# Two transformer layers on one core: full matmuls in column tiles, a square on GpSimd, Q's copies in one operation, a fifth pair

## The chip, the cores and the metric

The kernel runs on one NeuronCore of a Trainium2 chip. The core has a matrix engine (TensorE, PE in the profile; PEld is its loading of weights), VectorE (DVE), ScalarE (ACT), GpSimd (POOL) and the DMA queues, of which SyncE (SP) issues most. The metric is device time in microseconds (us), the median of several executions.

## The reference

Two identical layers, each an attention block and a feed-forward block, on 2048 rows of 512 columns in bf16. Both passes use the same weights.

```python
x = A_x                                   # [1, 2048, 512]
x = x + attention(layernorm(x), wqkv, wo)  # 32 heads of 16 columns
x = x + relu(layernorm(x) @ w1) @ w2       # w1 [512, 1792], w2 [1792, 512]
x = x + attention(layernorm(x), wqkv, wo)
x = x + relu(layernorm(x) @ w1) @ w2

# attention, for each head:
scores = (q @ k.T) * 16 ** -0.5            # 2048 x 2048
o = softmax(scores) @ v
```

There are 2 x 32 x 2048 x 2048 exponentials, 268 million. With 128 partitions working side by side that is 2,097,152 columns of one element per partition.

## The kernel before

Keys lie on the partitions. One matmul makes 128 keys x 512 queries of scores for one head; heads have only 16 columns, so four matmuls of 32 rows each (a head and its neighbour, with Q's copy masked so that the neighbour counts zero) sit in the array side by side. Three such blocks fill a slot of three PSUM banks (`ps_s`), and there are two slots in turn. A block of scores then goes one of two ways.

Most go through ScalarE's exponential, a whole slot of 1536 columns at once, or 1024 columns if VectorE takes the third block:

```python
ex = nc.scalar.activation(
    out=eb[:, 0 : place[m]], in_=b[:, 0 : place[m]], func=ACTF.Exp,
    scale=1.0 / (LOG2E * UNIT),
)
if half is not None:
    dve_block(half, taken, b[:, place[m] : W * QS], ex, recent)
```

The third block of some slots goes to VectorE, which makes the exponential by bit arithmetic. Two blocks make a pair. The scores become 16-bit integers that read as bf16 are a straight-line approximation (`lin`), once per block. Then a chain works on the whole pair of 1024 columns: it takes the mantissa (`step`), squares it (`power`, in the tile `cube`), takes the exponent (again into `step`), and multiplies. `lin`, `step` and `cube` all go to the second matmul with the values, which adds them up.

```python
first = nc.vector.tensor_scalar(                 # dve_block, once per block, reads PSUM
    out=lin[which][:, half * QS : (half + 1) * QS], in0=src, scalar1=EXP_BIAS,
    scalar2=0.0, op0=ALU.add, op1=ALU.max,
)
...
def bits(keep, put):                             # chain, once per pair
    nc.vector.tensor_scalar(
        out=stair, in0=line, scalar1=keep, scalar2=put, op0=ALU.bitwise_and,
        op1=ALU.bitwise_or,
    )

mantissa = stair.bitcast(BF16)
steps = (
    (342, lambda: bits(0x7F, 0x3F80)),
    (609, lambda: nc.vector.tensor_mul(out=power, in0=mantissa, in1=mantissa)),
    (342, lambda: nc.vector.tensor_scalar(       # left out for most pairs
        out=power, in0=power, scalar1=CUBE, scalar2=None, op0=ALU.mult)),
    (342, lambda: bits(0x7F80, 0)),
    (609, lambda: nc.vector.tensor_mul(
        out=power.bitcast(BF16), in0=power, in1=line.bitcast(BF16))),
)
```

How many pairs are lent to VectorE is decided while the program is built. The kernel's Python keeps a model of when each engine will be free (the first numbers in `steps` are nanoseconds of VectorE) and writes the instructions of each engine in the order that the model finds. A new pair is begun only if fewer than `NP` pairs are under way and its chain (`CHAIN`) would end in time:

```python
elif (not pairs or pair_no[0] + 1 - pairs[0]["n"] < NP) and (...):
    queued = sum(t["cost"] for t in dve_q if "chain" in t)
    ...
    ends = max(now_dve[0] + others, now_pe[0] + 2600.0) + SPREAD * (queued + CHAIN)
```

All other matmuls (Q, K, V, the output projection and the feed-forward block) go between those of attention and use the whole 128 x 128 array. Q is copied out of PSUM twice, with one mask for each of the two heads that share 32 rows.

```python
nc.tensor.matmul(out, lhsT, rhs, start=i % k == 0, stop=i % k == k - 1)   # mm_group

nc.tensor.matmul(                                # pv: values, four column tiles of 32
    ps_o[32 * g : 32 * g + 32, 0 : sg["w"]],
    values[:, 4 * sg["T"] + g, 2 * e : 2 * e + 32],
    rhs, start=g not in sg["begun"], stop=not sg["rem"][g],
    tile_position=(0, 32 * g), skip_group_check=True,
)

def q_masked(n, b, e, w=QS):
    return nc.vector.tensor_scalar(
        out=qbuf[n % 2][e][:, 0:w], in0=b, scalar1=qmask[e][:, 0:1], scalar2=None,
        op0=ALU.mult,
    )
```

GpSimd has little to do: it sets constants at the start, refines the layernorm's reciprocal square root on tiles of 4 columns, and issues the DMAs that spread a row of sums over partitions.

Of the kernel before, what the change touches and what calls it, by code (L numbers as in the profile page):

```python
# [11 lines left out]
FP32 = mybir.dt.float32  # L12
BF16 = mybir.dt.bfloat16
# [4 lines left out]
ALU = mybir.AluOpType  # L18
# [6 lines left out]
def kernel(  # L25
# [10 lines left out]
    nc = tc.nc  # L36
    P = 128
# [12 lines left out]
    QS = 512  # L50
    NQS = S // QS
    TPC = QS // P
    NT = 8
    SCALE = float(DH) ** -0.5
# [11 lines left out]
    LOG2E = 1.4426950408889634  # L66
    UNIT = 128.0
    EXP_BIAS = (127.0 - math.log2(SUM)) * UNIT
    CHAIN = 2500.0
    NP = 4  # L70
    NC = 3
    THIRD = (8, 9, 10, 11)

# [1 line left out]
    SWITCH = 105.0  # L75
# [3 lines left out]
    C_LAG, R_LAG, U_LAG = 3600.0, 10500.0, 3000.0  # L79
    VLAG = 1  # L80
    RSTD_LAG = 5000.0
    AHEAD = (8.0, 8.0)
    LATE = 0.0
    MID = 2
# [15 lines left out]
    def sb(shape, dt, name):  # L100
        return persist.tile(shape, dt, name=name)

    ident = sb([P, P], BF16, "ident")
    mask = [sb([P, 1], FP32, f"mask{e}") for e in range(2)]
    qmask = [sb([P, 1], FP32, f"qmask{e}") for e in range(2)]
    wqkv = sb([P, NDC, 3 * D], BF16, "wqkv")
    wo = sb([P, NDC, D], BF16, "wo")
    w1buf = [sb([P, NDC, P], BF16, f"w1_{n}") for n in range(NW1)]
# [16 lines left out]
    va2 = [sb([P, 2, H // 2, PW], BF16, f"vaug0_{n}") for n in range((NKB - TPC) // 2)]  # L125
# [11 lines left out]
    ot = [sb([P, QS], BF16, f"ot{t}") for t in range(NT)]  # L137
# [9 lines left out]
    acc0 = [x[:].bitcast(FP32).rearrange("p a b -> p (a b)") for x in htp]  # L147
    acc0.append(kt1[:].bitcast(FP32).rearrange("p a b -> p (a b)"))
    ebuf = [sb([P, W * QS], BF16, f"e{n}") for n in range(NE)]
    qbuf = [[sb([P, QS], BF16, f"q{n}_{e}") for e in range(2)] for n in range(2)]  # L150
    ubuf = [sb([P, QS], FP32, f"u{n}") for n in range(NU)]
    rbuf = [sb([P, QS], FP32, f"r{n}") for n in range(NU)]
    cbuf = [sb([P, QS // 32], FP32, f"c{n}") for n in range(NU)]
    xnbuf = [sb([P, D], BF16, f"xn{n}") for n in range(TPC)]
    stats = [sb([P, nc.vector.BN_STATS_DIM], FP32, f"stats{n}") for n in range(2)]
    mv = [sb([P, TPC, nc.vector.BN_AGGR_DIM], FP32, f"mv{n}") for n in range(2)]
    va_ = [sb([P, TPC], FP32, f"va{n}") for n in range(2)]
    ya_ = [sb([P, TPC], FP32, f"ya{n}") for n in range(2)]
    ta_ = [sb([P, TPC], FP32, f"ta{n}") for n in range(2)]
    warm = sb([P, 1], FP32, "warm")  # L160

    ps_s = [psum.tile([P, W, QS], FP32, name=f"ps_s{n}") for n in range(2)]
# [54 lines left out]
    def uses(ins, bank, makes=None, needs=None):  # L217

        tile, w = bank
        log = users.setdefault(tile, deque(maxlen=40))
        for other, ow, made_there in log:
            if (
                ow != w and other.engine != ins.ins.engine
                and (needs is None or made_there != needs)
            ):
                tc.declare_no_dep(ins.ins, other, reason="different PSUM banks")
        log.append((ins.ins, w, makes))
# [2 lines left out]

    now_pe = [0.0]
    now_dve = [0.0]
    mode = [None]
    busy = [0.0]
    bank_free = [0.0]
# [2 lines left out]
    def mark(key, engine="dve", lag=0.0):  # L240
        made[key] = (engine, (now_pe if engine == "pe" else now_dve)[0] + lag)

    def at(keys, engine):
# [10 lines left out]
            t = max(t, when)  # L254
        return t

    def pe_start(kind, ready=0.0):
        return max(now_pe[0] + (SWITCH if mode[0] != kind else 0.0), ready)

    def pe_run(kind, units, ready=0.0):  # L260
        now_pe[0] = pe_start(kind, ready) + units * MM
        mode[0] = kind
        busy[0] += units * MM

    def dve_run(cost, ready=0.0):
        now_dve[0] = max(now_dve[0], ready) + cost
# [33 lines left out]

    def do_piece():
        c, fn, ready = cur.popleft()
        pe_run("f", c, ready)
        fn()
        owed[0] -= c

# [111 lines left out]
    def mm_group(mms, fin, makes, deps, per=1, cost=EVAC, after=None, wide_by=QS, sums=1):  # L418


        hold = {}
        pieces = []
        n = len(mms)
        for a in range(0, n, per):

            def piece(a=a):
                if a == 0:
                    hold["b"] = bank()[:, 0 : sums * wide_by]
                b = hold["b"]
                for i in range(a, min(a + per, n)):  # L430
                    lhsT, rhs = mms[i]
                    k = n // sums
                    out = b[:, i // k * wide_by : (i // k + 1) * wide_by]
                    nc.tensor.matmul(out, lhsT, rhs, start=i % k == 0, stop=i % k == k - 1)  # L434
                if a + per >= n:
                    put_evac(cost, lambda: fin(b))
                    if after:
                        after()

            pieces.append((min(per, n - a) * wide_by / QS, piece))  # L440
        return group(pieces, makes, deps)
# [51 lines left out]
    def ln_newton(tag):  # L493

        n = ln_n(tag)
        a, y, t1 = va_[n][:], ya_[n][:], ta_[n][:]
        for _ in range(3):
            nc.gpsimd.tensor_mul(out=t1, in0=y, in1=y)
            nc.gpsimd.tensor_mul(out=t1, in0=t1, in1=a)
            nc.gpsimd.tensor_scalar(  # L500
                out=t1, in0=t1, scalar1=-0.5, scalar2=1.5, op0=ALU.mult, op1=ALU.add
            )
            nc.gpsimd.tensor_mul(out=y, in0=y, in1=t1)
# [117 lines left out]
            (wqkv[:, c, T * P : (T + 1) * P], xnT[xj][:, c, a : a + w]) for c in range(NDC)  # L621
        ]

    def q_masked(n, b, e, w=QS):
        return nc.vector.tensor_scalar(  # L625
            out=qbuf[n % 2][e][:, 0:w], in0=b, scalar1=qmask[e][:, 0:1], scalar2=None,
            op0=ALU.mult,
        )

    def q_group(n, l, j, T):  # L630
        xj, _, w = columns(l, j)
        cost = 133 + 1.045 * w

        def fin(b):
            q_masked(n, b, 0, w)
            evac.appendleft((cost, 0.0, lambda: (q_masked(n, b, 1, w), mark(("q", n)))))

        return mm_group(
            q_mms(l, j, T), fin, [("q", n)], each(TPC, "xnT", ("ln1", l, xj)), cost=cost,
            wide_by=w,  # L640
        )
# [151 lines left out]
    def finish_segment(sg, last):  # L793
# [40 lines left out]

        def mul(a, w):
            nc.vector.scalar_tensor_tensor(  # L836
                out=ot[t][:, at_column + a : at_column + a + w], in0=u[:, a : a + w], scalar=mask[e][:, 0:1],
                in1=r[:, a : a + w], op0=ALU.mult, op1=ALU.mult,
            )
            for i in range(a // P, (a + w) // P):  # L840
                mark(("ot", l, j, t, i))
# [189 lines left out]
    def chain(p):  # L1031
        key, n = p["key"], p["n"]
        line, stair, power = lin[n % NP][:], step[n % NC][:], cube[n % NC][:]

        def bits(keep, put):
# [3 lines that stand above are left out]
            )  # L1039

        mantissa = stair.bitcast(BF16)
        p["scaled"] = all(
            ("third", sg["l"], kb) in made for us in p["blocks"] for sg, kb, g in us
        )
        steps = (
            (342, lambda: bits(0x7F, 0x3F80)),
            (609, lambda: nc.vector.tensor_mul(out=power, in0=mantissa, in1=mantissa)),  # L1047
            (342, lambda: nc.vector.tensor_scalar(
                out=power, in0=power, scalar1=CUBE, scalar2=None, op0=ALU.mult)),
            (342, lambda: bits(0x7F80, 0)),  # L1050
            (609, lambda: nc.vector.tensor_mul(  # L1051
                out=power.bitcast(BF16), in0=power, in1=line.bitcast(BF16))),
        )
        nos = (0, 1, 3, 4) if p["scaled"] else range(5)
        for n, after in zip(nos, (None,) + tuple(nos)):
            cost, fn = steps[n]
            k = key + (n,) if n + 1 < len(steps) else key
            early = [("added", p["n"] - NC)] if p["n"] > NC else []
            task(cost, fn, [k], [key + (after,)] if n else early)
            maker[k]["chain"] = p  # L1060
# [11 lines left out]
    idle_matmuls(18)  # L1072
    for e in range(2):
        nc.vector.tensor_reduce(
            out=mask[e][:],
            in_=ident[:].rearrange("p (g e d) -> p e g d", g=4, e=2)[:, e],
            op=ALU.add, axis=mybir.AxisListType.XY,
        )
        nc.vector.tensor_scalar(
            out=qmask[e][:], in0=mask[e][:], scalar1=SCALE * LOG2E * UNIT, scalar2=None,  # L1080
            op0=ALU.mult,
        )
    for i in range(TPC):
# [24 lines left out]
    uses(nc.scalar.copy(out=ktp[0][0][0][:], in_=b), in_bank[0])  # L1108
    mark(("k", 0, 0, 0))
    b = plain(q_mms(0, 0, 0))  # L1110
    for e in range(2):
        uses(q_masked(0, b, e), in_bank[0])
    mark(("q", 0))
    for kb in range(2):
        b = plain(v_mms(kb))
# [57 lines left out]
    while units:  # L1173
# [123 lines left out]
        for _ in range(times):  # L1297
            pe_run("s", 1, s_ready)
            for a, (sg, kb, g) in sorted(zip(place, now), key=in_turn):
                kt = ktp[sg["l"]][sg["T"]][kb // TPC]  # L1300
                kc = (kb % TPC) * P
                nc.tensor.matmul(  # L1302
                    b[:, a : a + sg["w"]],
                    kt[32 * g : 32 * g + 32, kc : kc + P],
                    qbuf[sg["n"] % 2][sg["e"]][32 * g : 32 * g + 32, 0 : sg["w"]],
                    start=True, stop=True, tile_position=(32 * g, 0),
                )
        m = len(now) - len(taken)
# [160 lines left out]
```

The softmax here doesn't subtract the row's maximum and nothing guards it: scores larger than these inputs give would overflow.

## Time and profile before

| | us |
|---|---|
| median of 3 executions | 1614.96 |
| lowest, highest | 1613.95, 1618.53 |
| span of the profiled execution | 1611.5 |
| exponentials on ScalarE run from | 16.8 to 1577.9 |
| granted TensorE clock (mean) | 0.997 |

A busy time in the profile is the time in which an engine had an instruction under way. Instructions overlap at their ends, so the sum of single durations is larger than the busy time of the group. A matmul's duration includes its way through the array, and four that sit side by side count once each. In a line of a group, the number after the bar is the busy time in us, then the mean duration of one in ns, then the idle time of the engine before them and what ended it. Line numbers are those of the kernel before: L1302 are the score matmuls, L901 the ones with the values, L434 the full-array ones, L1311 the exponential, L995 the step `lin`, L1036 both bit operations, L1047 the square, L1051 the last multiplication, L625 Q's copies.

### The profile page before, as it was taken

To read this page: it belongs to the slowest core of one execution; us is meant where nothing else is said; L and a number is where in the kernel's file an instruction comes from. 1 tells how busy PE (TensorE), PEld (TensorE's weight loads), DVE (VectorE), ACT (ScalarE), POOL (GpSimd) and SP (SyncE) were. 2 spreads that over 40 slices of the span, in tenths; PEclk is the share of its full clock that TensorE was granted. 3 is DMA by queue.
4 is the path that set the end of the run, shared out by engine and by line. 5 is a ranking of instruction groups with operands and counts; after the bars stand their busy time and mean duration, and the time that the engine had idled before them with its cause. 6 is when DMAs were issued, how large, how long until landed. Compare 5 with 4: busy or idle time off the path is not lost.

```text
span 1611.5 us, 35252 instructions
## 1 busy us (share of the span) xinstructions
PE 1451.6 (90%) x14667; PEld 508.9 (32%) x14863; DVE 1496.8 (93%) x3007; ACT 1566.0 (97%) x1387; POOL 93.8 (6%) x279
## 2 busy tenths in 40 slices
PE   8888888999989999899998998888989999899997
PEld 3222222322222222222222222222333333344444
DVE  7669999999999999999898998999999999999994
ACT  6999999999999999999999999999999999999993
POOL 2000001001010011000100000001001010010100
PEclk9999999999999999999999999999999999999999
DMA  5000000210002100021000100000210111121223
GB/s 164 1 1 2 2 2 10 46 28 12 5 18 45 21 15 9 12 47 25 9 1 17 31 1 1 2 3 9 44 30 16 26 29 36 22 48 36 47 46 73
DMA packets 113889, 39.97 MB, mean 25 GB/s; under 512 B 103328, under 2 KB 111264, under 8 KB 113728
## 3 DMA queue, kind: packets, MB, share of 16 engines
q1 hardware_dynamic: 101696, 26.21, 7.1%
q0 software_dynamic: 10688, 10.18, 3.4%
q8 instruction: 116, 1.90, 0.5%
q10 hardware_dynamic: 1344, 1.31, 0.2%
q14 instruction: 45, 0.37, 0.1%
HBM read 24.38 MB, written 2.10 MB: 16 GB/s over the span
## 4 chain that ended last, share of the span: by engine, by line
ACT 78%; PE 11%; DVE 7%; issue 3%; DMA 1%; ACTq 0%; DVEq 0%
ACT e L1311 78%; PE ps_s L1302 4%; PE ps_o L901 3%; PE ps_f L434 3%; DVE lin L995 2%; DVE step L1036 1%; PE ps_s L1365 1%; DVE cube L1047 1%; DVE cube L1051 1%; DVE stats L465 0%; DVE ht L682 0%; DVE q L625 0%; DVE ot L836 0%; DVE x L708 0%; DMA c<-u 0%
## 5 line engine op out<-in xcount | busy, mean ns | idle before, releaser
L1311 ACT ACTIVATE e<-ps_s 128x1024 bf16<-128x1024 f32 (+1 forms) x1366 | 1554.8, 1367 | 6.6 <-PE ps_s L1302 4.7
L1302 PE MATMUL ps_s<-q,ktp 32*128 32x512 bf16 (+1 forms) x6060 | 601.2, 341 | 106.7 <-ACT e L1311 84.7
L901 PE MATMUL ps_o<-e,vaug 128*32 128x512 bf16 (+1 forms) x4284 | 494.7, 345 | 11.3 <-DVE u L823 4.8
L995 DVE TENSOR_SCALAR lin<-ps_s 128x512 int16<-128x512 f32 x662 | 452.6, 686 | 35.8 <-PE ps_s L1302 30.4
L1302 PEld LDWEIGHTS <-ktp 32*128 32x128 bf16 x6060 | 189.9, 91 | 504.5 <-issue 375.6
L1036 DVE TENSOR_SCALAR step<-lin 128x1024 int16<-128x1024 int16 x662 | 262.9, 420 | 3.3 <-PE ps_o L901 0.6
L901 PEld LDWEIGHTS <-vaug 128*32 128x32 bf16 x6004 | 161.5, 94 | 302.2 <-issue 291.5
L1047 DVE TENSOR_TENSOR cube<-step 128x1024 f16<-128x1024 bf16 x331 | 225.9, 685 | 2.7
L1051 DVE TENSOR_TENSOR cube<-cube,lin 128x1024 bf16<-128x1024 f16 x331 | 225.5, 682 | 0.0
L901 PE MATMUL ps_o<-step,vaug 128*32 128x512 bf16 (+1 forms) x836 | 143.2, 340 | 0.3 <-issue 0.3
L901 PE MATMUL ps_o<-cube,vthird 128*32 128x512 bf16 (+1 forms) x788 | 138.2, 337 | 0.6 <-issue 0.3
L901 PE MATMUL ps_o<-lin,vaug 128*32 128x512 bf16 (+1 forms) x836 | 127.4, 338 | 4.1 <-DVE u L823 2.8
L434 PE MATMUL ps_f<-xnT,w 128*128 128x512 bf16 (+1 forms) x446 | 116.9, 345 | 5.6 <-issue 2.5
L434 PE MATMUL ps_f<-w,ht 128*128 128x512 bf16 x334 | 104.8, 384 | 5.6 <-issue 4.3
L850 POOL DMA_DIRECT2D r<-u x52 | 37.5, 721 | 1165.9 <-DVE step L1036 424.3
L434 PE MATMUL ps_f<-xnT,wqkv 128*128 128x512 bf16 (+1 forms) x288 | 82.3, 359 | 6.4 <-issue 2.5
L682 DVE TENSOR_SCALAR ht<-ps_f 128x512 bf16<-128x512 f32 x103 | 70.7, 687 | 3.2 <-PE ps_f L434 3.0
L434 PE MATMUL ps_f<-wo,ot 128*128 128x512 bf16 x206 | 65.4, 384 | 3.0 <-issue 1.9
L625 DVE TENSOR_SCALAR q<-ps_f,qmask 128x512 bf16<-128x512 f32 (+1 forms) x102 | 64.8, 661 | 3.1 <-PE ps_f L434 3.0
L434 PEld LDWEIGHTS <-w 128*128 128x128 bf16 x504 | 39.1, 97 | 60.0 <-issue 50.6
L836 DVE SCALAR_TENSOR_TENSOR ot<-u,mask,r 128x512 bf16<-128x512 f32 (+2 forms) x82 | 51.3, 627 | 1.1
L901 PEld LDWEIGHTS <-vthird 128*32 128x32 bf16 x788 | 39.8, 95 | 32.8 <-issue 30.1
(91 smaller groups left out, 609.8 us busy)
## 6 DMA issues: line engine op xcount, KB each, us to landing
w<-in_B_w_dram SPq DMA_DIRECT2D x140, 128.0 KB
r<-u POOLq DMA_DIRECT2D x25, 256.0 KB, 7.1
r<-u POOLq DMA_DIRECT2D x27, 128.0 KB, 4.5
out_dram<-x SPq DMA_DIRECT2D x16, 128.0 KB
x<-in_A_x_dram SPq DMA_DIRECT2D x14, 128.0 KB
w<-in_B_w_dram SPq DMA_DIRECT2D x1, 1792.0 KB
wqkv<-in_A_wqkv_dram ACTq DMA_DIRECT2D x2, 512.0 KB
c<-u SPq DMA_DIRECT2D x48, 8.0 KB
```

The costliest lines, as they stand in the source:

```text
L434: nc.tensor.matmul(out, lhsT, rhs, start=i % k == 0, stop=i % k == k - 1)
L625: return nc.vector.tensor_scalar(out=qbuf[n % 2][e][:, 0:w], in0=b, scalar1=qmask[e][:, 0:1], scalar2=None, op0=ALU.mult,)
L682: nc.vector.tensor_scalar(out=out, in0=sums, scalar1=0.0, scalar2=None, op0=ALU.max)
L836: nc.vector.scalar_tensor_tensor(out=ot[t][:, at_column + a : at_column + a + w], in0=u[:, a : a + w], scalar=mask[e][:, 0:1], in1=r[:, a ...
L850: nc.gpsimd.dma_start(out=r[:, 0:width], in_=bass.AP(tensor=sums.tensor, offset=sums.offset, ap=[list(sums.ap[0]), [0, 32], [1, width]],),)
L901: nc.tensor.matmul(ps_o[32 * g : 32 * g + 32, 0 : sg["w"]], values[:, 4 * sg["T"] + g, 2 * e : 2 * e + 32], rhs, start=g not in sg["begun" ...
L995: first = nc.vector.tensor_scalar(out=lin[which][:, half * QS : (half + 1) * QS], in0=src, scalar1=EXP_BIAS, scalar2=0.0, op0=ALU.add, op1 ...
L1036: nc.vector.tensor_scalar(out=stair, in0=line, scalar1=keep, scalar2=put, op0=ALU.bitwise_and, op1=ALU.bitwise_or,)
L1047: (609, lambda: nc.vector.tensor_mul(out=power, in0=mantissa, in1=mantissa)),
L1051: (609, lambda: nc.vector.tensor_mul(out=power.bitcast(BF16), in0=power, in1=line.bitcast(BF16))),
L1302: nc.tensor.matmul(b[:, a : a + sg["w"]], kt[32 * g : 32 * g + 32, kc : kc + P], qbuf[sg["n"] % 2][sg["e"]][32 * g : 32 * g + 32, 0 : sg[" ...
L1311: ex = nc.scalar.activation(out=eb[:, 0 : place[m]], in_=b[:, 0 : place[m]], func=ACTF.Exp, scale=1.0 / (LOG2E * UNIT),)
```

## The change

There are four parts.

1. Full-array matmuls become four matmuls of 32 columns each, in the mode that the matmuls with the values use, so that the array needn't change its mode between the two kinds.
2. The square of every pair's mantissa goes from VectorE to GpSimd. That frees VectorE to take more pairs from ScalarE.
3. Q's two masked copies become one operation, with a mask of two columns, spread over 2 x 512 elements.
4. Five pairs may be under way instead of four, for the way over GpSimd and back takes longer. Small tiles are put together to find the room. `CHAIN` falls by the square's cost.

```diff
-    CHAIN = 2500.0
-    NP = 4
+    CHAIN = 1900.0
+    NP = 5
...
+    POOL_HOP = 200.0
+    SQUARE = 2450.0
...
+    MODE = {None: 0, "s": 1, "v": 2, "f": 2, "t": 3}
+
     def pe_start(kind, ready=0.0):
-        return max(now_pe[0] + (SWITCH if mode[0] != kind else 0.0), ready)
+        return max(now_pe[0] + (SWITCH if MODE[mode[0]] != MODE[kind] else 0.0), ready)
...
+    def pool_run(cost):
+        now_pool[0] = max(now_pool[0], now_dve[0] + POOL_HOP) + cost
+        return now_pool[0] + POOL_HOP - now_dve[0]
...
-                    nc.tensor.matmul(out, lhsT, rhs, start=i % k == 0, stop=i % k == k - 1)
+                    for g in range(4):
+                        cols = slice(32 * g, 32 * g + 32)
+                        nc.tensor.matmul(
+                            out[cols], lhsT[:, cols], rhs, start=i % k == 0,
+                            stop=i % k == k - 1, tile_position=(0, 32 * g),
+                            skip_group_check=True,
+                        )
...
-    def q_masked(n, b, e, w=QS):
-        return nc.vector.tensor_scalar(
-            out=qbuf[n % 2][e][:, 0:w], in0=b, scalar1=qmask[e][:, 0:1], scalar2=None,
-            op0=ALU.mult,
+    def q_masked(n, b, w=QS):
+        return nc.vector.tensor_mul(
+            out=qbuf[n % 2][:, :, 0:w],
+            in0=b.rearrange("p (e q) -> p e q", e=1).to_broadcast((P, 2, w)),
+            in1=qmask.rearrange("p (e q) -> p e q", q=1).to_broadcast((P, 2, w)),
         )
...
         mantissa = stair.bitcast(BF16)
+
+        def square():
+            nc.gpsimd.tensor_mul(out=power, in0=mantissa, in1=mantissa)
+            mark(key + (1,), lag=pool_run(SQUARE))
...
-            (609, lambda: nc.vector.tensor_mul(out=power, in0=mantissa, in1=mantissa)),
+            (0, square),
```

Left out here: the tiles `mask`, `qmask`, `va_`, `ya_` and `ta_`, which become parts of shared tiles, the two halves of `qbuf`, which become one tile, and the places that read them.

More of the change, by code (lines that the diff above doesn't have):

```diff
@@ L103 @@
     ident = sb([P, P], BF16, "ident")
-    mask = [sb([P, 1], FP32, f"mask{e}") for e in range(2)]
-    qmask = [sb([P, 1], FP32, f"qmask{e}") for e in range(2)]
+    masks = sb([P, 4], FP32, "masks")
+    mask = [masks[:, e : e + 1] for e in range(2)]
+    qmask = masks[:, 2:4]
     wqkv = sb([P, NDC, 3 * D], BF16, "wqkv")
@@ L149 @@
     ebuf = [sb([P, W * QS], BF16, f"e{n}") for n in range(NE)]
-    qbuf = [[sb([P, QS], BF16, f"q{n}_{e}") for e in range(2)] for n in range(2)]
+    qbuf = [sb([P, 2, QS], BF16, f"q{n}") for n in range(2)]
     ubuf = [sb([P, QS], FP32, f"u{n}") for n in range(NU)]
@@ L156 @@
     mv = [sb([P, TPC, nc.vector.BN_AGGR_DIM], FP32, f"mv{n}") for n in range(2)]
-    va_ = [sb([P, TPC], FP32, f"va{n}") for n in range(2)]
-    ya_ = [sb([P, TPC], FP32, f"ya{n}") for n in range(2)]
-    ta_ = [sb([P, TPC], FP32, f"ta{n}") for n in range(2)]
+    va2 = sb([P, 2, TPC], FP32, "va")
+    va_ = [va2[:, n] for n in range(2)]
+    ya2 = sb([P, 2, TPC], FP32, "ya")
+    ya_ = [ya2[:, n] for n in range(2)]
+    ta2 = sb([P, 2, TPC], FP32, "ta")
+    ta_ = [ta2[:, n] for n in range(2)]
     warm = sb([P, 1], FP32, "warm")
@@ L234 @@
     now_dve = [0.0]
+    now_pool = [0.0]
     mode = [None]
@@ L302, in do_piece @@
         c, fn, ready = cur.popleft()
-        pe_run("f", c, ready)
+        pe_run("t" if c == 1.3 else "f", c, ready)
         fn()
@@ L495, in ln_newton @@
         n = ln_n(tag)
-        a, y, t1 = va_[n][:], ya_[n][:], ta_[n][:]
+        a, y, t1 = va_[n], ya_[n], ta_[n]
         for _ in range(3):
@@ L631, in q_group @@
         xj, _, w = columns(l, j)
-        cost = 133 + 1.045 * w
+        cost = 90 + 2.09 * w
         def fin(b):
-            q_masked(n, b, 0, w)
-            evac.appendleft((cost, 0.0, lambda: (q_masked(n, b, 1, w), mark(("q", n)))))
+            q_masked(n, b, w)
+            mark(("q", n))
         return mm_group(
@@ L836, in mul @@
             nc.vector.scalar_tensor_tensor(
-                out=ot[t][:, at_column + a : at_column + a + w], in0=u[:, a : a + w], scalar=mask[e][:, 0:1],
+                out=ot[t][:, at_column + a : at_column + a + w], in0=u[:, a : a + w], scalar=mask[e],
                 in1=r[:, a : a + w], op0=ALU.mult, op1=ALU.mult,
@@ L1074 @@
         nc.vector.tensor_reduce(
-            out=mask[e][:],
+            out=mask[e],
             in_=ident[:].rearrange("p (g e d) -> p e g d", g=4, e=2)[:, e],
@@ L1079 @@
         nc.vector.tensor_scalar(
-            out=qmask[e][:], in0=mask[e][:], scalar1=SCALE * LOG2E * UNIT, scalar2=None,
+            out=qmask[:, e : e + 1], in0=mask[e], scalar1=SCALE * LOG2E * UNIT, scalar2=None,
             op0=ALU.mult,
@@ L1110 @@
     b = plain(q_mms(0, 0, 0))
-    for e in range(2):
-        uses(q_masked(0, b, e), in_bank[0])
+    uses(q_masked(0, b), in_bank[0])
     mark(("q", 0))
@@ L1304 @@
                     kt[32 * g : 32 * g + 32, kc : kc + P],
-                    qbuf[sg["n"] % 2][sg["e"]][32 * g : 32 * g + 32, 0 : sg["w"]],
+                    qbuf[sg["n"] % 2][32 * g : 32 * g + 32, sg["e"], 0 : sg["w"]],
                     start=True, stop=True, tile_position=(32 * g, 0),
```

## The prediction

> **What bounds the kernel now.** I read the busy shares and the chain first, then the groups by form, three windows, the waits, and short timelines of VectorE (DVE) beside GpSimd (POOL). The page:
>
> ```profile
> PE 1451.6 (90%) x14667; PEld 508.9 (32%) x14863; DVE 1496.8 (93%) x3007; ACT 1566.0 (97%) x1387; POOL 93.8 (6%) x279
> ...
> ACT 78%; PE 11%; DVE 7%; issue 3%; DMA 1%; ACTq 0%; DVEq 0%
> ```
>
> ScalarE (ACT) is the bound. The windows (us, then PE, PEld, DVE, ACT, POOL busy) cut the span where the exponentials begin and end:
>
> ```profile
> 0.00:16.80 16.80, 12.56 (x60) 5.50 (x61) 13.15 (x42) 4.42 (x7) 2.41 (x35) 1.00 0.78 252
> 16.80:1577.90 1561.10, 1412.88 (x14453) 488.84 (x14645) 1471.18 (x2931) 1554.85 (x1366) 91.40 (x244) 1.00 0.10 21
> 1577.90:1611.50 33.60, 26.18 (x162) 14.59 (x160) 12.43 (x35) 6.72 (x14) 0.00 (x0) 0.97 0.29 71
> ```
>
> In the middle window ACT is idle for 1561.10 - 1554.85 = 6.25 us, POOL is nearly empty, and DVE idles for only 90 us. The groups that matter:
>
> ```profile
> L1311 ACT ACTIVATE e<-ps_s 128x1536 bf16<-128x1536 f32 x703 | 1052.1, 1573 | 4.5 <-PE ps_s L1302 2.8 <-PE ps_o L901 1.2
> L1311 ACT ACTIVATE e<-ps_s 128x1024 bf16<-128x1024 f32 x662 | 717.7, 1148 | 2.1 <-PE ps_s L1302 1.9 <-PE ps_o L901 0.2
> L995 DVE TENSOR_SCALAR lin<-ps_s 128x512 int16<-128x512 f32 x662 | 452.6, 686 | 35.8 <-PE ps_s L1302 30.4
> L1036 DVE TENSOR_SCALAR step<-lin 128x1024 int16<-128x1024 int16 x662 | 262.9, 420 | 3.3 <-PE ps_o L901 0.6
> L1047 DVE TENSOR_TENSOR cube<-step 128x1024 f16<-128x1024 bf16 x331 | 225.9, 685 | 2.7
> L1051 DVE TENSOR_TENSOR cube<-cube,lin 128x1024 bf16<-128x1024 f16 x331 | 225.5, 682 | 0.0
> ```
>
> A full exponential has 1536 columns, one with a block lent to DVE has 1024; 331 pairs of blocks are lent. 512 columns of ACT cost 1573 - 1148 = 425 ns. PE is not the bound, as the waits show (total us, times, longest): it waits for ACT 18 times as long as ACT waits for it.
>
> ```profile
> PE ps_s L1302 <- ACT e L1311: 84.7, 234, 1.0
> ...
> ACT e L1311 <- PE ps_s L1302: 4.7, 14, 0.6
> ```
>
> The last view decides my prediction. Start, duration, engine, operation, at two places:
>
> ```profile
> 457.12 0.68 DVE L1051 TENSOR_TENSOR cube<-cube,lin 128x1024 bf16<-128x1024 f16 x1
> 457.72 0.68 DVE L1047 TENSOR_TENSOR cube<-step 128x1024 f16<-128x1024 bf16 x1
> ```
>
> ```profile
> 457.30 0.56 POOL L498 TENSOR_TENSOR ta<-ya 128x4 f32<-128x4 f32 x1 [11.75 <-DVE ya L480]
> 457.94 0.52 POOL L499 TENSOR_TENSOR ta<-ta,va 128x4 f32<-128x4 f32 x1
> ...
> 461.12 0.20 POOL L498 TENSOR_TENSOR ta<-ya 128x4 f32<-128x4 f32 x1
> ```
>
> A four-element POOL multiplication takes 0.20 us when DVE works on PSUM (at 461.12), but at 457.30 it ends at 457.86, 0.06 us after the DVE multiplication that ends at 457.80; the next ends 0.06 us after the DVE operation that ends at 458.40. They do not share, they exclude each other. The other direction is seen once or twice, beside a DMA that POOL issues:
>
> ```profile
> 1263.44 0.61 DVE L1036 TENSOR_SCALAR step<-lin 128x1024 int16<-128x1024 int16 x1
> ```
>
> ```profile
> 1263.15 0.68 POOL L850 DMA_DIRECT2D r<-u  x1 [11.38 <-DVE cube L1051]
> ```
>
> Here a bit operation takes 0.61 us instead of 0.42 and ends only 0.22 us after POOL is done (1264.05 against 1263.83).
>
> [...] rounds of one kind start 0.21 to 0.23 us apart (703.55, 703.78, 703.99), those of different kinds 0.32 to 0.33 us (700.16, 700.49).
>
> **The change part by part**, counted in the static listing of both kernels.
>
> ACT: 703 full and 662 short exponentials become 645 and 720 (one of 512 columns in both), 360 pairs in place of 331. The number of instructions stays 1366, and 58 of them lose 512 columns: 58 x 0.425 = 24.7 us less on the engine that sets the end. With all else hidden: 1615 - 24.7 = 1590 us. At best the 6 us of ACT's waits go too.
>
> Column tiles: each full-array matmul becomes four of 32 columns. A round of four column tiles with their four weight loads already passes in 0.21 us (the rounds above), as long as one full matmul, so the work costs nothing. Changes of mode fall from 3302 to 2645: 657 x 0.105 = 69 us of PE, but PE only waits more for ACT. Worth 0 to 6 us.
>
> Q's copies: the pair took 1.40 us (703.48) with the two starts 0.66 us apart; one operation of 1024 columns from PSUM should take about 1.14 us from start to start, at the 0.6 us per 512 of other PSUM reads. 36 x 0.2 = 7 us of DVE, a few more from the half-wide ones.
>
> The square: DVE loses 331 operations of 0.60 us (start to start: 457.12 to 457.72), 199 us. The 29 extra pairs add 29 x (2 x 0.61 + 2 x 0.34 + 0.60) = 73 us. Summing all rows by their start-to-start times, DVE's total falls by 130 us: 1471 - 130 = 1341 us in the middle window. Were POOL free to work beside it, DVE would have 200 us of slack.
>
> But POOL now holds the shared port 360 times[...]. DVE's operations that need it (720 bit operations of 0.34, 360 multiplications of 0.60, and the smaller ones on ot, xn) sum to 537 us. [...] I walked down the 360 places where a square is released: in 155 the next DVE operation itself needs the port and goes first; after it, the work from PSUM that DVE can do until it next needs the port is 1.09 us on average (a single 0.6 us operation is commonest). [...] DVE then needs 1341 + 420 = 1761 us, is the bound, and with the edges (16.8 + 33.6) the kernel takes 1811 us. Holding the port for 2.0 or 2.4 us instead gives 355 or 485 us of stalls, 1747 or 1877 us.
>
> The fifth pair hides the longer way over POOL (2.45 us and two hops), not a blocked engine: DVE works in order, so a stalled bit operation also holds back the step that frees the score bank, and PE and ACT with it.
>
> **The rivals.**
> A, ACT stays the bound (1585 to 1600 us): true if POOL's long operation takes the port only in short pieces. For it: none of DVE's multiplications beside POOL's small operations is stretched (longest 700 ns), and stalls of up to about 0.5 us a pair fit in the 200 us of slack. Against it: those operations move four elements, and the exclusive waits at 457 us.
> B, DVE becomes the bound through the shared port (1747 to 1877 us): the exclusion seen at 457 and 1263 us, and the budget above.
> C, POOL loses instead: squares wait until DVE leaves the port and finish late, and DVE then waits for POOL's semaphores at the second bit operation. This ends in the same engine; fewer squares early, later ones queued; 1650 to 1750 us.
> D, PE suffers under four times as many instructions for the full matmuls: the 0.21 us rounds speak against it; a few us at most.
>
> **Range and chances.** I give B with C 0.65, A 0.35. B alone would say about 1800; with C and a part of A the middle of all lies near 1750 us, which is my prediction, with a range of 1582 to 1880. Faster by over 2% needs less than 1583 us, below what A's 24.7 us can give without the waits: 0.06. Within 2%: 0.30. Slower: 0.64.
>
> **What would show it.** Right, if the second bit operation and the last multiplication last well over 0.42 and 0.68 us on average (by some 1 us in sum per pair), DVE's busy share passes ACT's, and ACT waits for PE, and PE for DVE's first step, by hundreds of us. [...] Wrong, if those DVE durations stay as they are: then 1590 us stands, and the port isn't held for the whole instruction. The count of 58 shorter exponentials and the 0.21 us of a tiled full matmul are checked by the groups.

## The result and the profile after

| | us |
|---|---|
| before, median | 1614.45 |
| changed, median (lowest to highest) | 1881.18 (1879.63 to 1884.38) |
| ratio, 95% interval | 1.165 (1.1623 to 1.1677) |

The change makes the kernel 16.5% slower, a microsecond above the upper end of the predicted range. The first lines of the page of the changed kernel, busy time by engine and then the chain that ended last:

```profile
PE 1574.8 (84%) x19836; PEld 543.6 (29%) x19836; DVE 1653.2 (88%) x2771; ACT 1578.3 (84%) x1385; POOL 791.0 (42%) x639
...
DVE 23%; PE 14%; ACT 5%; issue 2%; POOL 1%; DMA 1%; POOLq 0%; DVEq 0%; ACTq 0%
```

ScalarE, 97% busy before, is at 84%. The chain can be followed back over only 46% of the span here, so its shares can't be set beside the 78% of before; within these 46%, VectorE has half and ScalarE a ninth. But VectorE isn't at 100% either: it is idle for 1880.1 - 1653.2 = 227 us, more than before. No engine is full; they wait for each other. The groups, with lines numbered as in the changed kernel (L1334 the exponential, L1064 the square, L1056 the bit operations, L1075 the last multiplication):

```profile
L1334 ACT ACTIVATE e<-ps_s 128x1536 bf16<-128x1536 f32 x645 | 934.1, 1488 | 146.8 <-PE ps_s L1325 132.8 <-PE ps_o L921 11.9
L1334 ACT ACTIVATE e<-ps_s 128x1024 bf16<-128x1024 f32 x720 | 730.6, 1050 | 119.9 <-PE ps_s L1325 113.3 <-PE ps_o L921 3.2 <-ACT e L1334 0.3
L1064 POOL TENSOR_TENSOR cube<-step 128x1024 f16<-128x1024 bf16 x360 | 704.1, 1964 | 701.5 <-DVE step L1056 578.9 <-PE ps_o L921 68.3 <-PE ps_s L1325 42.4
L1015 DVE TENSOR_SCALAR lin<-ps_s 128x512 int16<-128x512 f32 x720 | 486.5, 681 | 90.4 <-PE ps_s L1325 85.8 <-ACT e L1334 1.8 <-issue 1.0
L1056 DVE TENSOR_SCALAR step<-lin 128x1024 int16<-128x1024 int16 x720 | 478.1, 684 | 30.2 <-POOL cube L1064 26.9 <-PE ps_o L921 1.6
L1075 DVE TENSOR_TENSOR cube<-cube,lin 128x1024 bf16<-128x1024 f16 x360 | 313.5, 872 | 0.0
```

The reader should compare two rows with their like of before. The bit operation goes from 420 to 684 ns on average and the multiplication from 682 to 872, though the instructions are the same; `lin`, which reads PSUM, stays at 681 (686 before). A stall beside a square is not idle time in this view: it lengthens the instruction that waits. And ScalarE's idle time before the exponential, 6.6 us before, is now 267 us, nearly all of it waiting for score matmuls.

One stall in the timeline, VectorE and then GpSimd (start, duration, engine, operation):

```profile
701.94 2.02 DVE L1056 TENSOR_SCALAR step<-lin 128x1024 int16<-128x1024 int16 x1
```

```profile
701.76 1.90 POOL L1064 TENSOR_TENSOR cube<-step 128x1024 f16<-128x1024 bf16 x1
```

The square ends at 703.66, the bit operation at 703.96; VectorE's next operation, a multiplication, starts only at 703.88. In the trace 163 bit operations, 51 multiplications and nine operations that write `xn` (the normalised rows) last over 60 ns longer than the median of their kind, 279 us in sum. The bit operations that met one square end 0.28 us after it (median 283 ns, the middle half within 1 ns), the multiplications 0.55 us after it. The distance is the same wherever they met it: a blocked operation gets on only once the square has ended. What the prediction calls the port is this exclusion; the traces show no more of it than whom it stops and for how long. It stops 14 operations that write `ot` and five that scale `cube` too (19 us over their medians in sum), but none of the 720 `lin` and no other operation of VectorE lasts 60 ns longer than the median of its kind. The squares are hardly held up in turn, with 1.96 us on average and 1.90 at the median, and VectorE idles only 27 us for them, so rival C of the prediction has little part.

### The profile page after: what moved, and what is told of

It is laid out like the page before. It is cut to its first block, busy times and chain, and to the rows that moved or that the text cites. A ratio compares the mean times of both kernels' runs of the same rounds, so it can differ in the third digit from the quotient of the medians.

```text
span 1880.1 us, 45948 instructions
## 1 busy us (share of the span) xinstructions
PE 1574.8 (84%) x19836; PEld 543.6 (29%) x19836; DVE 1653.2 (88%) x2771; ACT 1578.3 (84%) x1385; POOL 791.0 (42%) x639
## 5 line engine op out<-in xcount | busy, mean ns | idle before, releaser
L1334 ACT ACTIVATE e<-ps_s 128x1536 bf16<-128x1536 f32 (+1 forms) x1366 | 1568.4, 1256 | 266.7 <-PE ps_s L1325 246.1
L1064 POOL TENSOR_TENSOR cube<-step 128x1024 f16<-128x1024 bf16 x360 | 704.1, 1964 | 701.5 <-DVE step L1056 578.9
L1056 DVE TENSOR_SCALAR step<-lin 128x1024 int16<-128x1024 int16 x720 | 478.1, 684 | 30.2 <-POOL cube L1064 26.9
L1075 DVE TENSOR_TENSOR cube<-cube,lin 128x1024 bf16<-128x1024 f16 x360 | 313.5, 872 | 0.0
L449 PE MATMUL ps_f<-xnT,w 128*32 128x512 bf16 (+1 forms) x2016 | 159.5, 373 | 16.2 <-DVE ht L702 10.3
L449 PE MATMUL ps_f<-w,ht 128*32 128x512 bf16 x1624 | 161.4, 400 | 3.2 <-DVE x L728 1.7
L449 PE MATMUL ps_f<-xnT,wqkv 128*32 128x512 bf16 (+1 forms) x1312 | 116.9, 380 | 10.8 <-DVE ktp L594 3.6
L449 PE MATMUL ps_f<-wo,ot 128*32 128x512 bf16 x960 | 91.5, 399 | 4.3 <-DVE x L668 3.1
L449 PEld LDWEIGHTS <-w 128*32 128x32 bf16 x2016 | 60.3, 102 | 51.1 <-issue 36.2
L856 DVE SCALAR_TENSOR_TENSOR ot<-u,masks,r 128x512 bf16<-128x512 f32 (+2 forms) x82 | 63.8, 778 | 1.1
```

What stands on the lines that cost most here:

```text
L449: nc.tensor.matmul(out[cols], lhsT[:, cols], rhs, start=i % k == 0, stop=i % k == k - 1, tile_position=(0, 32 * g), skip_group_check=True,)
L856: nc.vector.scalar_tensor_tensor(out=ot[t][:, at_column + a : at_column + a + w], in0=u[:, a : a + w], scalar=mask[e], in1=r[:, a : a + w] ...
L1056: nc.vector.tensor_scalar(out=stair, in0=line, scalar1=keep, scalar2=put, op0=ALU.bitwise_and, op1=ALU.bitwise_or,)
L1064: nc.gpsimd.tensor_mul(out=power, in0=mantissa, in1=mantissa)
L1075: (609, lambda: nc.vector.tensor_mul(out=power.bitcast(BF16), in0=power, in1=line.bitcast(BF16))),
L1334: ex = nc.scalar.activation(out=eb[:, 0 : place[m]], in_=b[:, 0 : place[m]], func=ACTF.Exp, scale=1.0 / (LOG2E * UNIT),)
```

## The experiments

The kernel before took 1615.6 us beside the first four runs on the same chip, 1615.8 us beside the next four and 1617.7 us beside the last four. A run given without an interval is a single execution. Single executions of the kernel before went from 1610.7 to 1619.2 us, so a difference of a few us between two such runs says little.

**Less of the square, in the same order.** The first three take the changed kernel and alter the GpSimd instruction alone, so that every engine's order stays (`cube` is filled with ones at the start, for what is left out).

```diff
-            nc.gpsimd.tensor_mul(out=power, in0=mantissa, in1=mantissa)
+            nc.gpsimd.tensor_mul(out=power[:, 0:4], in0=mantissa[:, 0:4], in1=mantissa[:, 0:4])
```

> The changed kernel, instruction for instruction, but GpSimd squares only 4 of the 1024 columns (the other squares are left out, so the values are not the reference's). Theory P, the shared port is held through the whole square: the stalls vanish, bit operations go back to 0.42 us on average, ScalarE is the bound again, 1583 to 1600 us. Rival E, four times as many instructions for the full matmuls on TensorE and the lower clock are the cause: stays above 1800 us. Rival L, the way over GpSimd and back is too long: falls too, so this run alone doesn't tell L from P.

Measured: 1608.74 us. Its page and its two VectorE groups:

```profile
PE 1461.6 (91%) x19832; PEld 538.5 (34%) x19836; DVE 1368.3 (85%) x2771; ACT 1544.4 (96%) x1385; POOL 185.0 (12%) x642
```

```profile
L1058 DVE TENSOR_SCALAR step<-lin 128x1024 int16<-128x1024 int16 x720 | 285.3, 418 | 7.1 <-POOL cube L1066 3.5 <-PE ps_o L923 2.2
L1077 DVE TENSOR_TENSOR cube<-cube,lin 128x1024 bf16<-128x1024 f16 x360 | 244.9, 681 | 0.0
```

The durations are back at 418 and 681 ns. All of the 272 us between this run and the changed kernel hang on the width of one GpSimd instruction. Of rival E, the number of TensorE instructions is out, for it is the same here. The clock isn't: it rose too, from 0.918 to 0.979, so it may carry a part of what the stalls set off. VectorE's busy time is 1368.3 against 1653.2 us with the same instructions, so the stalls sum to 285 us. But 1608.7 is not the 1590 us that ScalarE's shorter exponentials promised.

With 512 columns instead of 4:

> As the changed kernel, but GpSimd squares 512 of the 1024 columns (the other half is left out). The order is the same. P: the port is held for about 0.95 us a pair; walking down VectorE's order gives 94 us of stalls against 200 us of slack, so 1595 to 1650 us; the bit operations average about 0.50 us. If time goes with the length of the square in a straight line between no square and the whole one: about 1735 us. E: above 1800 us.

Measured: 1666.49 us, above the range of P; the bit operations average 513 ns, the multiplications 751. VectorE is busy for 1463.3 us, so the stalls sum to 95 us, as the walk down the order said (94). The time, however, is 58 us above the run with 4 columns: slack hid 37 us of the 95.

**As late, but without the port.**

```diff
-            nc.gpsimd.tensor_mul(out=power, in0=mantissa, in1=mantissa)
+            for _ in range(7):
+                nc.gpsimd.tensor_mul(out=power[:, 0:4], in0=mantissa[:, 0:4], in1=mantissa[:, 0:4])
```

> As the changed kernel, but the square is seven chained GpSimd multiplications of 4 columns, 0.28 us apart as the small ones were before: as late as the whole square (1.96 us) with the port hardly held (the squares are left out). P: 1585 to 1615 us, bit operations at 0.42 us. L, the latency over GpSimd is what costs: 1800 us and more.

Measured: 1621.14 us, a little above the range of P and far from L; bit operations 418 ns, multiplications 681. The seven take 245 ns each, 1.7 us in all. The way over GpSimd costs some 12 us, little more than single executions differ. The rest, 260 us, goes with the port.

**The square back on VectorE.**

```diff
-    CHAIN = 1900.0
+    CHAIN = 2500.0
...
-            (0, square),
+            (609, lambda: nc.vector.tensor_mul(out=power, in0=mantissa, in1=mantissa)),
```

> The changed kernel with the square back on VectorE and CHAIN at 2500 again: column tiles, Q's copies in one operation and the fifth pair alone. The listing has 680 short exponentials (before 662): 18 x 0.425 = 7.7 us less of ScalarE. P and L: 1600 to 1612 us, clock 0.99. E: above 1700 us.

Measured: 1608.69 us, ratio to before 0.9957 (0.9942 to 0.9973). The rest of the change is a small gain.

**The granted clock.** In the trace of the changed kernel TensorE's granted clock is 0.50 for 310 us, in 52 stretches, and 1.00 in all the rest (mean 0.918; before, 11 us and 0.997). `FLOOR` in the kernel's model repeats score matmuls to keep TensorE busy; here it is raised from 0.56 to 1.0.

> The changed kernel with FLOOR at 1.0 instead of 0.56, which repeats score matmuls (8329 in the listing, 6095 before) to keep TensorE busy while it waits; 704 short exponentials instead of 720. Theory C, the stalls let TensorE fall to half its clock for 310 us and that makes a good part of the 266 us: the clock rises from 0.92 to 0.97 or more and the time falls by 40 us or more, to 1780 to 1840 us. Theory S, the stalls alone (285 us) make it and nothing absorbs them: within 20 us of 1881, whatever the clock.

Measured: 1906.64 us with a clock of 0.937, far from theory C and 6 us outside theory S. This doesn't settle the clock's part. It rose by a third of what was hoped, the schedule changed with it (704 short exponentials), and the repeats keep TensorE busy for 89 us more (1663.4 against 1574.8). A second try, on the kernel with 4-column squares:

> 4-column squares (the others left out) and FLOOR at 0.68: 710 short exponentials, 7192 score matmuls. The half-clock time falls from 71 us to under 15, and ScalarE's waits from 35 us to 15: 1588 to 1600 us. If the clock had no part in it: 1608 us or more.

Measured: 1608.63 us. The clock rose from 0.979 to 0.995 and the time is the same (1608.74). That doesn't show that the half clock costs nothing. ScalarE's idle time among the exponentials fell from 26.5 to 23.0 us, but with ten short exponentials fewer it works 2.8 us more, and the repeats keep TensorE busy for 37 us more (1498.3 against 1461.6). What the clock gave may have gone into the extra work. Two neighbouring windows of the run with 4-column squares (us, then PE, PEld, DVE, ACT, POOL busy, and the clock) show what half clock looks like:

```profile
142.21:155.86 13.65, 12.83 (x91) 2.57 (x88) 5.91 (x13) 8.27 (x8) 0.67 (x3) 0.50 0.01 1
155.86:172.93 17.07, 13.36 (x147) 3.94 (x143) 15.43 (x30) 15.73 (x15) 0.84 (x4) 1.00 0.01 2
```

In the first TensorE is busy almost throughout and ScalarE idles for 5.4 us.

**The full matmuls in one piece again**, with the square on GpSimd and then on VectorE (with `CHAIN` at 2500). The `MODE` that the kernel's model has for these matmuls goes back with them.

```diff
-                    for g in range(4):
-                        cols = slice(32 * g, 32 * g + 32)
-                        nc.tensor.matmul(
-                            out[cols], lhsT[:, cols], rhs, start=i % k == 0, ...
+                    nc.tensor.matmul(out, lhsT, rhs, start=i % k == 0, stop=i % k == k - 1)
```

> The changed kernel with the full-array matmuls in one piece, as before: the square on GpSimd, Q's copies in one operation and the fifth pair stay (714 short exponentials). If the square on GpSimd makes the loss and the column tiles have no part in it: 1850 to 1900 us. If the column tiles add to it: below 1830 us.

Measured: 1876.78 us. The column tiles have no part in the loss that can be seen.

> Square on VectorE and full-array matmuls in one piece: only Q's copies in one operation and the fifth pair remain of the change (676 short exponentials). If the column tiles bring nothing: 1605 to 1611 us, like the run with them (1608.7). [...] The half-clock time should be near the 11 us of the kernel before, not the 31 us of the run with column tiles, if freeing TensorE is what lets its clock fall.

Measured: 1624.35 us, ratio 1.006 (1.0037 to 1.0083), above what was expected: Q's copies and the fifth pair by themselves make the kernel a little slower. Beside the 1608.69 us of the same kernel with column tiles, the tiles are worth 15.7 us, and the small gain of the rest is theirs. The windows show where (us, then PE, PEld, DVE, ACT, POOL busy, from the first exponential to the last and then to the end). In one piece:

```profile
16.80:1587.20 1570.40, 1412.99 (x14449) 489.70 (x14635) 1475.13 (x2926) 1550.23 (x1366) 91.41 (x244) 1.00 0.10 21
1587.20:1621.10 33.90, 26.47 (x167) 14.64 (x159) 12.42 (x35) 6.79 (x14) 0.00 (x0) 0.98 0.29 71
```

In column tiles:

```profile
16.80:1578.40 1561.60, 1411.18 (x19631) 524.32 (x19629) 1480.91 (x2936) 1547.82 (x1366) 90.00 (x244) 0.99 0.11 22
1578.40:1607.70 29.30, 22.91 (x134) 12.55 (x133) 11.81 (x34) 5.55 (x13) 0.00 (x0) 0.92 0.24 59
```

ScalarE is idle for 20 us of the first stretch with full matmuls and for 14 us with tiles; its work is 2 us less; and the end is 4.6 us shorter. In the kernel before, feed-forward matmuls were still left when the exponentials had ended; in the trace with tiles the last output projection starts at once.

**Warmer, with the square on VectorE.**

> Square on VectorE, column tiles, Q's copies, fifth pair, and FLOOR at 0.68 instead of 0.56 (7212 score matmuls in the listing, 6192 without; 678 short exponentials). Theory C: the half-clock time falls from 31 us to below 10, ScalarE's waits from 18 us to 10, and the time to 1598 to 1605 us. If TensorE's extra work delays more than the clock gives: 1609 us or more.

Measured: 1606.78 us (14 executions, 1605.42 to 1614.05), ratio 0.9951 (0.9941 to 0.9962). It is the fastest median of all and beats both kernels, by half a per cent of the one before; from the run with `FLOOR` at 0.56 it can't be told apart, for the intervals overlap. Theory C expected 1605 us or less, its rival 1609 or more; the run decides for neither.

**Where VectorE's slack went.** VectorE idles 1606.9 - 1368.3 = 239 us in the run with 4-column squares. The next two put work into it that the kernel's model doesn't know, in even pieces: every pair's second bit operation is made twice, or three times, with the same result.

```diff
-            (342, lambda: bits(0x7F80, 0)),
+            (342, lambda: [bits(0x7F80, 0) for _ in range(2)]),
```

> The run with 4-column squares, and VectorE makes every pair's second bit operation twice (the same result again). That is some 0.42 us a pair, 150 us of VectorE work that the kernel's model knows nothing of, in small even pieces instead of a few long stalls. VectorE idles 235 us in the run without it. If slack on VectorE absorbs extra time of any kind: 1610 to 1640 us. If nothing absorbs it, because the queues move in step: 1608.7 + 150 = 1740 to 1770 us. A value between (1650 to 1700) says that part of it is absorbed.

> The same with the second bit operation made three times: some 0.84 us a pair, 300 us of even VectorE work, about as much as the 285 us of stalls in the changed kernel. If the stalls cost by their sum alone: 1860 to 1910 us, like the changed kernel. If even work is absorbed up to the slack and long stalls are not: 1680 to 1780 us.

Measured: 1661.00 us, where a part is absorbed, and 1827.08 us, between the two expectations. With the square's two runs this makes a table; both columns are differences to the run with 4-column squares, in us.

| run | more VectorE busy time | more time |
|---|---|---|
| second bit operation twice | 132 | 52 |
| three times | 284 | 218 |
| square of 512 columns (stalls) | 95 | 58 |
| square of 1024 columns (stalls) | 285 | 272 |

Of 239 us of idle time, even work filled 80 us in the first run and 66 in the second; stalls filled 37 and 13 us. What lies beyond costs its full length and somewhat more: 152 us more of even work cost 166, 190 us more of stalls 214. The even work made three times (284 us) is as much as the changed kernel's stalls, and costs 54 us less. The traces show where these 54 us lie. Counted here are the score columns that ScalarE and VectorE take per us, from the first exponential to the last, apart by the granted clock:

| run | us at 1.00 | columns per us | us at 0.50 | columns per us |
|---|---|---|---|---|
| 4-column squares | 1494 | 1361 | 67 | 944 |
| second bit operation three times | 1651 | 1199 | 130 | 905 |
| changed kernel (stalls) | 1527 | 1207 | 307 | 826 |

At full clock 284 us of even work and 285 us of stalls slow the kernel alike, to within 1%. What remains is the time at half clock, which is more than twice as long with the stalls. Had the changed kernel kept its pace of full clock throughout, it would have been some 97 us faster, which is an estimate from this table: 307 us less the 253,659 columns of that time at 1207 per us. The stalls come first, for without them the half clock shrinks to 67 us; how much of their cost it carries is shown by no run.

**A model that knows of the port.** The kernel's own scheduler was told not to place an operation that needs the port before the square has ended, if other work is ready, and its `SQUARE` was set from 2450 to 1900.

```diff
+    def when_ready(t):
+        ready = at(t["deps"], "dve")
+        return ready if ready is None or not t.get("port") else max(ready, port_free[0])
...
-        dve_run(t["cost"], at(t["deps"], "dve"))
+        dve_run(t["cost"], when_ready(t))
```

> The changed kernel with a model that knows of the port: VectorE's bit operations, multiplications and ot are not placed before GpSimd's square (1.9 us) has ended, if other work is ready. It lends fewer pairs (313; 626 short exponentials), which costs ScalarE 36 x 0.425 = 15 us against the kernel before, and walking down its order still gives 223 us of stalls. If order alone could save the square on GpSimd: below 1615 us. By the stalls: 1700 to 1830 us.

Measured: 1919.05 us, worse than the changed kernel and outside both expectations. The stalls did shrink, the idle time grew:

```profile
PE 1617.8 (84%) x20451; PEld 582.1 (30%) x20455; DVE 1397.2 (73%) x2535; ACT 1607.3 (84%) x1385; POOL 695.8 (36%) x592
```

```profile
L1022 DVE TENSOR_SCALAR lin<-ps_s 128x512 int16<-128x512 f32 x626 | 428.2, 686 | 241.5 <-PE ps_s L1333 223.4 <-ACT e L1342 8.6 <-issue 6.0
L1063 DVE TENSOR_SCALAR step<-lin 128x1024 int16<-128x1024 int16 x626 | 307.7, 520 | 41.1 <-POOL cube L1071 38.6 <-PE ps_o L928 2.4
```

The bit operations fall from 684 to 520 ns, but VectorE idles 242 us before `lin`, nearly all of it for scores (90 in the changed kernel). The order that avoids the port starves something else, and with 94 short exponentials fewer ScalarE has more to do. Whether a better order could make the square on GpSimd pay stays open; this one doesn't.

## Why the prediction was wrong

The direction and the mechanism (rival B) were right; the size was not, and the range ended at 1880.

*Right.* VectorE's time without stalls: 1341 us predicted for the middle stretch, and 1368.3 us for the whole span where the stalls are gone, 1343.3 of it in that stretch. Tiled full matmuls keep their pace: rounds of four start 216 ns apart at the median in the run with 4-column squares, like single full matmuls before (216 to 227 ns). Most of the signature came as described: longer bit operations and multiplications at the same count, by 2 x 264 + 190 = 718 ns a pair (some 1 us was named), and ScalarE waiting 246 us for score matmuls. TensorE's wait for the first step is smaller than the hundreds of us named: 59 us for `lin`, and 73 for the bit operations. The waits (us in total, times, longest), of which the first two came to less than 1 and to 3.0 us before:

```profile
PE ps_o L921 <- DVE step L1056: 73.4, 59, 4.1
PE ps_s L1325 <- DVE lin L1015: 58.7, 68, 3.5
...
ACT e L1334 <- PE ps_s L1325: 246.1, 281, 4.7
```

*Wrong, the step that failed:* "DVE then needs 1341 + 420 = 1761 us, is the bound, and with the edges (16.8 + 33.6) the kernel takes 1811 us." It holds two errors of opposite sign. The window of the changed kernel's exponentials:

```profile
16.80:1851.50 1834.70, 1540.11 (x19626) 526.16 (x19625) 1628.25 (x2696) 1568.39 (x1366) 788.54 (x604) 0.92 0.09 19
```

- The stalls are 285 us, not 420. The 420 were my estimate, for a length of the square that no trace of before shows; it takes 1.9 us (median 1.90), less than the 2.0 us that gave 355. A walk down the order with 1.9 us gives 321 us.
- VectorE is idle for 1834.7 - 1628.3 = 206 us in this window, where the sentence has none; 63 of them lie in the 307 us at half clock, which the prediction doesn't have either. The idle time is the term that broke the range: 1811 - 135 (stalls) + 206 (idle) + 2 (work) - 5 (a shorter end) = 1879 us.

The reason behind it was the word "bound". I let VectorE's stalls eat its 200 us of slack before they cost anything, and let it run without a gap afterwards. The even work shows that only 66 to 80 us of the slack can be had, and 13 to 37 for stalls. The waits fit this reason, which no run isolates: orders are fixed and there are only two slots of score banks, so a stalled VectorE holds back TensorE, which holds back ScalarE, and VectorE later waits for late scores itself (86 us for `lin`). How much the half clock adds to these waits stays open.

*Wrong, the floor of rival A.* "With all else hidden: 1615 - 24.7 = 1590 us" was never reached. With 4-column squares, where the bit operations take 418 ns again, the window of the exponentials is as long as before:

```profile
16.80:1577.70 1560.90, 1426.11 (x19616) 520.37 (x19616) 1343.28 (x2696) 1534.44 (x1366) 179.94 (x604) 0.98 0.11 22
```

ScalarE is busy 20.4 us less than before in this window (1534.44 against 1554.85) and idle 20.2 us more (26.46 against 6.25). All of its relief came back as waits. So even without the port the change would have been worth no more than the 6.8 us of this run, and most of those are the shorter end. Of the 26.5 us of idle time 17.5 lie in the 67 us at half clock (before, 1.6 us of 6.3), so the clock is a suspect. The warmer run doesn't clear it: it exchanged the half clock for more work.

*Wrong, the worth of the column tiles.* The fewer changes of mode were to bring 0 to 6 us, because TensorE would only wait more for ScalarE. What a change costs is seen in the starts of matmuls of 512 columns at full clock: before, a full one follows a round with the values after 329 ns (median of 189 places); in the changed kernel a tiled one does so after 228 ns (median of 21). The tiles brought 15.7 us: ScalarE's waits among the exponentials fell from 20 to 14 us (Q's copies and the fifth pair had raised them from the 6 us that the prediction counted on), and the end grew shorter by 4.6 us.

*The mixture.* I put 1750 between two peaks and so predicted a time that no mechanism gave. B by itself gave 1747 to 1877 us, with the idle time left out. That its upper end, for a hold of 2.4 us, lies 4 us from the measured time is luck: the hold was 1.9 us, and idle time made up for it.

## What to carry to other kernels

Before work goes to GpSimd, sum the time of its instructions and of the VectorE operations that they stop (here the bit operations, the multiplications, the scaling of `cube` and those that write `xn` and `ot`), walk down VectorE's order to the next such operation, and charge it the rest of the GpSimd instruction; in the trace, look for the stall in mean durations (here 684 ns in place of 420), not in idle time. Then charge nearly all of such stalls to the span: here 239 us of idle time hid no more than 13 to 37 us of them. And when the engine at the bound is relieved by a per cent or two, look first at who feeds it: here its waits gave back the whole gain.

## What the runs showed of the hardware beyond that

- GpSimd's 16-bit square of 1024 columns takes 1.90 us at the median, of 512 columns 1.04: 1.7 ns for each further column, and less in all than the 2.45 us that the changed kernel's `SQUARE` reckons with.
- Two squares in a row can keep a waiting VectorE operation out for both. A group of two squares on GpSimd and the bit operation beside it:

```profile
288.58 3.74 POOL L1064 TENSOR_TENSOR cube<-step 128x1024 f16<-128x1024 bf16 x2
```

```profile
288.89 3.73 DVE L1056 TENSOR_SCALAR step<-lin 128x1024 int16<-128x1024 int16 x1
```

The bit operation, 0.42 us long, starts during the first square and ends at 292.62, 0.30 us after the second. This happened six times; the longest bit operation took 4.41 us. In 17 other cases a bit operation got on between two squares.
- A GpSimd instruction that works on four columns delays no VectorE operation that the trace can show, even seven in a row (418 and 681 ns): there, 282 bit operations that begin beside a GpSimd instruction take 420 ns on average, the others 415 (five beside a DMA issue apart).
